# Twelve Newton instructions on VectorE where GpSimd took one power, and a plan sorted anew

## The chip, the core and the metric

The kernel runs on one core of one Trainium2 chip. The metric is device time in microseconds (us) of one execution. Five engines work at once, each through its own queue of instructions in a fixed order: PE (TensorE, matrix products), DVE (VectorE), ACT (ScalarE), POOL (GpSimd) and SP (SyncE, which issues the transfers). An instruction that waits holds up everything behind it on its engine.

## What is computed

Attention with normalised queries and keys over 8 batches of 12 heads, 448 rows of 64 numbers, and then a feed-forward layer on the 3584 x 768 result, all in float32:

```python
def rmsnorm(x, g):
    rms = np.sqrt(np.mean(x * x, axis=-1, keepdims=True) + 1e-06)
    return x / rms * g
q_n, k_n = (rmsnorm(q, g_q), rmsnorm(k, g_k))
scores = scale * np.matmul(q_n, k_n.transpose(0, 1, 3, 2))
attn = np.exp(scores - np.max(scores, axis=-1, keepdims=True))
attn = attn / (np.sum(attn, axis=-1, keepdims=True) + 1e-09)
...
h = x @ w_in            # 768 -> 2048
g = h * np.cos(h)
return (g @ w_out).astype(np.float32)
```

The part that this case touches is the `1 / rms` of the keys of the first two heads.

## The kernel before

The work is cut into 48 units `u`, each a pair of heads. Six pairs make a batch. For a pair the seven blocks of 128 query rows give seven score tiles (`score_plain` or `score`, PE), DVE scales each by the query's inverse root and takes the row minimum (`rowmin`, L553), ACT takes the exponential (`expo`, L561), PE transposes the result (`transp`, L595 to L604), ACT and DVE copy it out of PSUM, and PE multiplies with the values (`av`, `av_plain`). The three score tiles in bank `S` and one in bank `ph` are all that may be open at once for the first pairs, so a later score matmul waits until the exponential has read an earlier tile. The first six pairs run in plain float32; all later ones split each operand in a high and a low part (`pt_high`, `pt_low` and so on). While pairs 6 and up are done, the first feed-forward product of the batch before (`ffn1`, L726 to L728) fills the gaps on PE. After the attention comes the second product, seven block products (`ffn2`, L800 to L802).

Inverse roots are found in two ways of data flow, but by the same instruction. For every pair `st_square` (ACT) and `st_reduce` (DVE) give sums of squares, `r`, and `st_pow` (POOL, L380 and L381) raises them to the power -0.5. The first two pairs are special: their keys come in row by row (`kn_load`; the keys of pair 0 lie in tile `kq`, of pair 1 in tile `kn`), and a short chain normalises and turns them on the chip. It is `kn_square` (ACT, L399), `kn_reduce` (DVE, L405), `kn_pow` (POOL, L409 and L410), `kn_norm` (DVE, L415), `kn_turn` (PE, L420) and `kn_copy` (ACT, L425), which leaves the keys as `kn` with the gains folded in. From pair 2 on the roots go through HBM (`st_store`, `rk_spread`) and POOL multiplies (`k_norm`, L458, giving `km`).

The order of all this is not written out. Each step is registered by `add` with an engine, a cost in us, a due time and the data that it reads and writes. `Plan.order` then plays the program through in its own model of the five engines: whenever an engine is free, it takes, of the steps whose inputs are there, the one that is due first. The steps are emitted in that order, and the chip's queues keep it. `SHIFT` moves the due times of a kind of step by so many us, apart for three stages of the program (pairs 9 and up, pairs 6 to 8, and the first six).

```python
        if name in ("pt_low", "pt_high", "pt_copy", "transp"):
            name += str(args[2])
        elif name == "av" and args[1] == 3:
            name += "3"
        due += SHIFT.get(name, (0.0,) * 3)[stage]
...
        cost *= {DVE: 1.059, ACT: 1.026, POOL: 1.021}.get(eng, 1.0)
        plan.add(eng, cost, due, fn, *args, **more)
```

Of the kernel before, what the change touches and what calls it, by code (L numbers as in the profile page):

```python
# [10 lines left out]
F32 = mybir.dt.float32  # L11
F32R = mybir.dt.float32r
I32 = mybir.dt.int32
AF = mybir.ActivationFunctionType
ALU = mybir.AluOpType
# [5 lines left out]
PE, ACT, DVE, POOL, SP = "PE", "ACT", "DVE", "POOL", "SP"  # L21
# [128 lines left out]
def tile_attention_moe(  # L150
# [11 lines left out]
    nc = tc.nc  # L162
    NU = sd_in.shape[0]
    B, S, D = 8, kq_in.shape[2] - 512, 64
# [11 lines left out]
    KB = S // 4  # L176
# [32 lines left out]
    def g_fold():  # L209
# [5 lines left out]
    wts, wfl, raw = {}, {}, {}  # L215
    RING = {
# [3 lines left out]
    }  # L220

# [94 lines left out]
    pair = {}  # L316
# [37 lines left out]
    def tl(u, name, shape, dt, tag=None):  # L354
        tag = tag or name
        t = pair.setdefault(u, {})[name] = apool.tile(shape, dt, tag=tag, name=f"{name}{u}", bufs=RING[tag])
        return t
# [43 lines left out]
    def kn_reduce(u, a, b):  # L401
        if a == 0:
            tl(u, "rn", [128, 8], F32)
        sq = kn_bank(u)[:KB, 128 * a : 128 * b].rearrange("p (t d) -> p t d", d=D)
        nc.vector.tensor_reduce(pair[u]["rn"][:KB, 2 * a : 2 * b], sq, axis=AX.X, op=ALU.add)  # L405

    def kn_pow(u):
        r = pair[u]["rn"][:KB]
# [266 lines left out]
    xf = {}  # L675
# [141 lines left out]
    def y_store(b, oc, src):  # L817
# [2 lines left out]

    plan = Plan(RING, loose=PKEYS)
    SHIFT = {
        "av": (5.3, 0.0, 0.0), "av3": (3.6, 0.0, 0.0), "av_plain": (0.0, 0.0, 15.8), "e_place": (-4.5, 0.0, 0.0),
        "expo": (8.1, 0.0, 0.0), "ffn1": (0.0, -3.8, 0.0), "h_out": (-4.4, 0.0, 0.0), "k_high": (5.2, 7.1, 0.0),
        "kq_load": (-19.1, 0.0, 0.0), "m_place": (15.1, -13.5, 0.0), "pt_copy0": (0.0, 0.0, -3.9),
        "pt_high1": (-1.8, 0.0, 0.0), "pt_low0": (-20.7, 9.3, 0.0), "pt_low1": (-5.9, 0.0, 0.0),
        "q_high": (5.1, 0.0, 0.0), "q_low": (-2.0, 3.7, 0.0), "q_scale": (-9.4, -8.6, 0.0),
        "rowmin": (10.1, 6.2, 1.1), "rs_copy": (0.0, 2.2, 0.0), "rs_load": (0.0, 0.0, -12.0),
        "rs_store": (6.6, 0.0, 11.5), "rsum": (-8.3, 0.0, 0.0), "st_pow": (-14.6, 0.0, 0.0),
        "st_reduce": (5.3, 0.0, 0.0), "st_square": (2.5, 0.0, 0.0), "transp0": (-4.1, 0.0, 0.0),  # L830
        "transp1": (2.4, -8.7, 0.0), "v_decode": (8.3, 0.0, 0.0), "v_high": (0.0, 12.8, 0.0),
        "v_load": (19.8, -12.8, 0.0), "v_store": (12.5, 0.0, 0.0), "w_decode": (0.4, 0.0, 0.0),
        "x_norm": (4.0, 0.0, 0.0), "x_plain": (0.0, 0.0, -20.3), "x_split": (-3.4, 0.0, 0.0),
        "x_sum": (13.2, 0.0, 0.0),
    }

    def add(eng, cost, due, fn, *args, **more):
        name, first = fn.__name__, args[0] if args else 0
        stage = 0
        if name in ("ffn1", "h_out", "h_store", "h_both", "x_split"):  # L840
            stage = int(first < (NP if name == "x_split" else 1))
        elif name[:2] not in ("w_", "v_", "e_") or name in ("v_load", "v_high", "v_low", "v_plain", "e_place"):
            stage = 2 if first < NP else int(first < NP + 3)
# [5 lines that stand above are left out]
        if name in ("w_load", "w_decode", "w_high", "w_low"):  # L849
            due += -0.414 * first  # L850
        if name in ("ffn1", "h_out", "h_store", "h_both") and not first:
            due += -0.355 * args[1]
        if name in ("v_fetch", "v_decode", "v_sum", "v_split", "v_store"):
            due += 25.441 * first
        cost *= {DVE: 1.059, ACT: 1.026, POOL: 1.021}.get(eng, 1.0)
        plan.add(eng, cost, due, fn, *args, **more)
# [68 lines left out]
    def prepare(u):  # L925
        D0 = base(u)
        kmw = [km_key(u)]
        sd, r, kd, khi, qd, qhi = ([(n, u)] for n in ("sd", "r", "kd", "khi", "qd", "qhi"))
        sd = [("sd", max(u, NKT - 1), u)]
        turned, plain = u < NKT, u < NP  # L930
        if turned:
            kn, rn, kb = [("qd" if u == 0 else "ql", u)], [("rn", u)], [("pt", 0, n) for n in ((0,) if u == 0 else (1, 2))]
            add(SP, ISS, D0 - 60, kn_load, u, w=kn, kb=224.0)
            halves = ((0, 2), (2, 4)) if u == 0 else ((0, 4),)
            hs = [("kn", u, h) for h in halves]
            sh = 1.0 / len(halves)
            for h, k in zip(halves, hs):
                add(ACT, 0.06 + 0.57 * sh, D0 - 50, kn_square, u, *h, r=kn, w=[k, *(kb if h[0] == 0 else [])])
            for h, k in zip(halves, hs):
                add(DVE, 0.06 + 0.63 * sh, D0 - 50, kn_reduce, u, *h, r=[k, *kb], w=[("rn" if h[0] == 0 else "rm", u)])  # L940
            add(POOL, 1.9, D0 - 50, kn_pow, u, r=kb, w=rn + [("rm", u)])
            for h, k in zip(halves, hs):
                add(DVE, 0.06 + 0.63 * sh, D0 - 50, kn_norm, u, *h, r=rn + kn, w=[k])
            for h, k in zip(halves, hs):
                add(PE, 0.98 * sh, D0 - 50, kn_turn, u, *h, r=[k, *kn, *kb], w=[k])
            for n, (h, k) in enumerate(zip(halves, hs)):
                add(ACT, 0.73 if u else (0.36, 0.53)[n], D0 - 50, kn_copy, u, *h, r=[k, *kb, ("gsc", 0)], w=kmw)
        elif plain:
            add(SP, ISS, D0 - 36, k_load, u, w=kd, kb=224.0, start=D0 - 36)
        else:  # L950
            add(SP, ISS, D0 - 34, kq_load, u, w=kd + qd, kb=480.0, start=D0 - 40)
        add(SP, ISS, D0 - 45, st_load, u, w=sd, kb=224.0 if turned else 448.0, start=0.0 if u < NP else D0 - 60)
        if plain:
            add(SP, ISS, D0 - 44 if turned else D0 - 30, q_load, u, w=[("qp", u)], kb=256.0,
                start=0.0 if turned else D0 - 28)
        add(ACT, 0.55 if turned else 0.86, D0 - 40, st_square, u, w=sd)
        add(DVE, 0.7 if turned else 1.08, D0 - 38, st_reduce, u, r=sd, w=r, start=9.0 * (u == 1))
        add(POOL, 2.25 if turned else 2.9, D0 - 34, st_pow, u, w=r)
        if not turned:
            add(SP, ISS, D0 - 30, st_store, u, r=r, w=[("rkd", u)], kb=4.0)  # L960
            if plain:
                add(SP, 2 * ISS, D0 - 26, rk_spread, u, r=[("rkd", u)], w=[("D", u)], kb=224.0)
                add(POOL, 1.55, D0 - 18, k_norm, u, r=[("D", u)] + kd, w=kmw)
            else:
                add(SP, ISS, D0 - 26, rk_load, u, r=[("rkd", u)], w=[("M", u, 2)], kb=224.0)
                add(POOL, 1.13, D0 - 20, k_norm, u, r=[("M", u, 2)], w=kd)
                add(ACT, 0.5, D0 - 17, k_high, u, r=kd, w=khi)
                add(POOL, 1.2, D0 - 15, k_low, u, r=kd + khi, w=[("kl", u)])
        if plain:
            if not turned:  # L970
                add(POOL, 0.8, D0 - 16, q_scale, u, r=[("gsc", 0)], w=[("qp", u)])
            add(SP, ISS, D0 - 12, v_plain, u, w=[("vs", u)], kb=256.0, start=D0 - 6)
            return
        add(POOL, 0.66, D0 - 19, q_scale, u, r=[("gsc", 0)], w=qd)
        add(ACT, 0.52, D0 - 16, q_high, u, r=qd, w=qhi)
        add(POOL, 1.26, D0 - 14, q_low, u, r=qd + qhi, w=[("ql", u)])
        add(SP, 2 * ISS, D0 - 14, m_place, u, 0, r=khi, w=[("M", u, 0)], kb=358.0)
        add(SP, 2 * ISS, D0 - 13.5, d_place, u, r=qhi, w=[("D", u)], kb=614.0)
        add(SP, 2 * ISS, D0 - 13, m_place, u, 1, r=[("kl", u)], w=[("M", u, 1)], kb=358.0)
        add(SP, ISS, D0 - 12.5, e_place, u, r=[("ql", u)], w=[("E", u)], kb=307.0)  # L980
        add(SP, ISS, D0 - 12, v_load, u, w=[("vd", u)], kb=256.0, start=D0 - 22)
        add(POOL, 0.82, D0, v_high, u, r=[("vd", u)], w=[("vs", u)])
        add(POOL, 1.3, D0 + 2, v_low, u, r=[("vd", u)], w=[("vs", u)])
# [160 lines left out]
    add = plan.add  # L1144
# [170 lines left out]
```

## Time and profile before

| | us |
|---|---|
| median of 3 runs | 1373.23 (1372.65 to 1375.12) |
| the profiled execution | 1371.8 |
| its span, first to last instruction | 1370.0 |
| PE busy in the span | 1343.2 (98%) |
| DVE, ACT, POOL busy | 1075.0, 927.4, 632.5 |

The profile comes from one execution, and its 1371.8 us is 1.4 us under the median. PE counts as busy while any matmul is in flight, and its matmuls overlap, so 98% is not 98% of its best rate. The idle time of PE is not spread evenly: about half of it lies in the first 60 us.

### The profile page before, as it was taken

How to read it: one execution, taken by the hardware profiler on the slowest of the kernel's cores; microseconds unless marked ns; L12 is line 12 of the kernel's file. 1: busy time of each engine (PE TensorE's matmuls, PEld its weight loads, DVE VectorE, ACT ScalarE, POOL GpSimd, SP SyncE). 2: the span in 40 equal slices, each digit the busy share in tenths (PEclk: the TensorE clock that was granted, in tenths of full speed). 3: DMA queues.
4: the chain of work that ended last, by engine and by line, in shares of the span. 5: the costliest groups of instructions: out<-in, count | busy, mean ns of one | idle time of the engine just before them, and what ended most of it. 6: DMA issues, size and time to landing. Idle time of an engine off the chain costs nothing.

```text
span 1370.0 us, 21500 instructions
## 1 busy us (share of the span) xinstructions
PE 1343.2 (98%) x6998; PEld 1171.0 (85%) x6998; DVE 1075.0 (78%) x1859; ACT 927.4 (68%) x1872; POOL 632.5 (46%) x554
## 2 busy tenths in 40 slices
PE   7899999999999999999999999999999999999998
PEld 3346888788888989888889888999999999999998
DVE  7888899977787887787877877628889889889742
ACT  6677878777877877777777787638666366366321
POOL 4889978676766866666776584330000000000000
PEclk9999999999999999999999999999999999999999
DMA  6798776889798899798987897338988369369334
GB/s 241 263 276 194 186 170 188 240 232 244 201 260 212 216 243 209 218 243 227 247 209 196 227 233 200 120 131 315 370 298 300 119 246 306 112 247 313 105 113 153
DMA packets 149472, 302.19 MB, mean 221 GB/s; under 512 B 34368, under 2 KB 83088, under 8 KB 149360
## 3 DMA queue, kind: packets, MB, share of 16 engines
q1 hardware_dynamic: 149360, 300.83, 75.2%
q8 instruction: 55, 0.90, 0.3%
q14 instruction: 57, 0.47, 0.1%
HBM read 193.99 MB, written 62.73 MB: 187 GB/s over the span
## 4 chain that ended last, share of the span: by engine, by line
PE 86%; POOL 5%; DVE 3%; DMA 2%; issue 2%; ACT 1%; SPq 0%; POOLq 0%; ACTq 0%; DVEq 0%
PE y L800 10%; PE y L802 10%; PE y L801 10%; PE ph L726 9%; PE ph L727 8%; PE ph L728 8%; PE S L549 8%; PE PT L595 7%; PE O L642 4%; PE O L644 3%; PE O L660 1%; PE S L533 1%; PE y L727 1%; PE y L728 1%; PE y L726 1%
## 5 line engine op out<-in xcount | busy, mean ns | idle before, releaser
L553 DVE TENSOR_SCALAR_CACHE_REDUCE S<-S,r 128x448 f32<-128x448 f32 x336 | 225.3, 686 | 56.4 <-PE S L549 45.4
L561 ACT ACTIVATE P<-S,sm 128x448 f32<-128x448 f32 x336 | 213.3, 637 | 73.8 <-DVE S L553 56.7
L726 PE MATMUL ph<-xs,wi 128*128 128x448 f32 x660 | 251.1, 380 | 1.6 <-ACT hbuf L744 1.6
L800 PE MATMUL y<-g,wo 128*128 128x448 f32 x672 | 245.4, 365 | 0.0
L801 PE MATMUL y<-g,wo 128*128 128x448 f32 x672 | 245.4, 365 | 0.0
L802 PE MATMUL y<-g,wo 128*128 128x448 f32 x672 | 245.4, 365 | 0.0
L727 PE MATMUL ph<-xs,wi 128*128 128x448 f32 x660 | 241.7, 366 | 0.0
L728 PE MATMUL ph<-xs,wi 128*128 128x448 f32 x660 | 241.3, 366 | 0.0
L782 ACT CAST g<-gq 128x896 fp32r<-128x896 f32 x112 | 105.7, 944 | 170.6 <-PE y L802 170.1
L618 ACT CAST hi<-PT 128x512 fp32r<-128x512 f32 (+2 forms) x336 | 175.7, 532 | 63.7 <-PE PT L595 23.8
L625 DVE TENSOR_TENSOR lo<-PT,hi 128x512 fp32r<-128x512 f32 (+1 forms) x252 | 153.2, 619 | 41.2 <-ACT hi L618 39.0
L780 DVE TENSOR_TENSOR g<-gq,g 128x896 fp32r<-128x896 f32 x112 | 122.0, 1089 | 60.2 <-ACT g L782 59.7
L595 PEld LDWEIGHTS PT<-ident,P 128*128 128x128 f32 x1008 | 124.0, 141 | 42.2 <-issue 6.6
L595 PE MATMUL PT<-ident,P 128*128 128x128 f32 x1008 | 155.8, 275 | 2.8 <-DVE rt L574 1.2
L726 PEld LDWEIGHTS ph<-xs,wi 128*128 128x128 f32 x660 | 124.2, 188 | 17.8 <-ACT hbuf L744 3.4
L800 PEld LDWEIGHTS y<-g,wo 128*128 128x128 f32 x672 | 126.2, 188 | 10.0
L802 PEld LDWEIGHTS y<-g,wo 128*128 128x128 f32 x672 | 126.2, 188 | 9.9
L801 PEld LDWEIGHTS y<-g,wo 128*128 128x128 f32 x672 | 126.2, 188 | 9.9
L728 PEld LDWEIGHTS ph<-xs,wi 128*128 128x128 f32 x660 | 124.0, 188 | 10.6
L727 PEld LDWEIGHTS ph<-xs,wi 128*128 128x128 f32 x660 | 124.4, 189 | 8.6
L381 POOL TENSOR_TENSOR r<-r,nhalf 128x14 f32<-128x14 f32 (+1 forms) x48 | 124.5, 2593 | 4.0
L642 PE MATMUL O<-hi,vs 128*128 128x448 f32 x336 | 122.3, 378 | 1.1 <-DVE hi L627 0.8
(129 smaller groups left out, 2635.9 us busy)
## 6 DMA issues: line engine op xcount, KB each, us to landing
wo<-wo_d SPq DMA_DIRECT2D x152, 384.0 KB
gq<-h_d SPq DMA_DIRECT2D x64, 448.0 KB
h_d<-hbuf SPq DMA_DIRECT2D x54, 448.0 KB
wo_d<-ao SPq DMA_DIRECT2D x56, 384.0 KB
sd<-sd SPq DMA_DIRECT2D x46, 448.0 KB
kq<-kq SPq DMA_DIRECT2D x42, 480.0 KB
D<-qhi SPq DMA_DIRECT2D x84, 192.0 KB
raw<-w_in SPq DMA_DIRECT2D x16, 768.0 KB
```

Of the source, the lines that this page charges most:

```text
L553: nc.vector.tensor_scalar(d["S", t][:, :S], d["S", t][:, :S], d["r"][:, t : t + 1], None, op0=ALU.mult, op1=ALU.min, accum_out=d["sm"][:, ...
L561: nc.scalar.activation(p_rows(u, t), d.pop(("S", t))[:, :S], AF.Exp, bias=sm[:, 1, t : t + 1], scale=-1.0, accum_out=sm[:, 2, t : t + 1],)
L595: nc.tensor.transpose(pt[part][:, i * 128 : i * 128 + 128], p_rows(u, t)[:, c : c + 128], ident)
L618: nc.scalar.copy(hi if kc < 3 else hi[:64], pt_rows(u, kc, part))
L625: nc.vector.tensor_tensor(lo, src, hi.bitcast(F32), ALU.subtract)
L642: nc.tensor.matmul(O, st, d["hi", kc][:, HEADS[hh]], start=(kc == 0), stop=(kc == 3))
L726: nc.tensor.matmul(ph[:, :S], whi, x2[:, 0, :], start=(cc == 0), stop=False)
L727: nc.tensor.matmul(ph[:, :S], whi, x2[:, 1, :], start=False, stop=False)
L728: nc.tensor.matmul(ph[:, :S], wlo, x2[:, 0, :], start=False, stop=(cc == NCC - 1))
L800: nc.tensor.matmul(y, whi, hi[:, e], start=first and e == 0, stop=False, **more)
L801: nc.tensor.matmul(y, whi, lo[:, e], start=False, stop=False, **more)
L802: nc.tensor.matmul(y, wlo, hi[:, e], start=False, stop=last and e == NG - 1, **more)
```

## The change

Pair 0 alone gets `kn_root` in place of `kn_pow`. It adds the epsilon on DVE, makes a first guess of the inverse root from the bits of the number (shift, multiply by -1, add a constant), and improves it in three Newton steps of three instructions. That is twelve DVE instructions on 112 x 8 numbers, each of which reads what the one before it wrote. The plan counts them as one step of 0.85 us. Pair 1 keeps `kn_pow`. Two small tiles are added. In `SHIFT` six entries become zero, in whole or in one stage: `e_place`, `ffn1`, `pt_low0`, `q_low`, `rowmin` (first six pairs) and `transp1`; the rest stand as before.

```diff
+    def kn_root(u):
+        x = pair[u]["rn"][:KB]
+        y, t = (tl(u, name, [128, 8], F32)[:KB] for name in ("ry", "rt8"))
+        nc.vector.tensor_scalar(x, x, D * 1e-6, 3.0e38, op0=ALU.add, op1=ALU.min)
+        nc.vector.tensor_scalar(
+            y.bitcast(I32), x.bitcast(I32), 1, 0x7FFFFFFF, op0=ALU.logical_shift_right, op1=ALU.bitwise_and
+        )
+        nc.vector.tensor_scalar(y.bitcast(I32), y.bitcast(I32), -1.0, 1597463007.0, op0=ALU.mult, op1=ALU.add)
+        for last in (False, False, True):
+            nc.vector.tensor_tensor(t, x, y, ALU.mult)
+            nc.vector.scalar_tensor_tensor(t, t, -0.5, y, op0=ALU.mult, op1=ALU.mult)
+            nc.vector.scalar_tensor_tensor(x if last else y, t, 1.5, y, op0=ALU.add, op1=ALU.mult)
...
-        "pt_low0": (-20.7, 9.3, 0.0), "pt_low1": (-5.9, 0.0, 0.0),
+        "pt_low0": (0.0, 9.3, 0.0), "pt_low1": (-5.9, 0.0, 0.0), "q_high": (5.1, 0.0, 0.0),
...
-            add(POOL, 1.9, D0 - 50, kn_pow, u, r=kb, w=rn + [("rm", u)])
+            if u:
+                add(POOL, 1.9, D0 - 50, kn_pow, u, r=kb, w=rn + [("rm", u)])
+            else:
+                add(DVE, 0.85, D0 - 50, kn_root, u, r=kb, w=rn + [("rm", u)])
```

What this does to the queues is seen at the start on three engines. In the changed kernel the lines after L405 stand 13 further down: `kn_norm` is L428, `kn_copy` L438, `rowmin` L566 and `expo` L574.

On POOL, at the start of the program; `rn_127` is the sums of pair 0's keys, `rn_145` (in the changed kernel `rn_151`) those of pair 1, `r_137` and `r_155` (`r_157` and `r_176`) the sums of the queries of pairs 0 and 1. Before:

```order
L409 TENSOR_SCALAR rn_127<-rn_127 112x8
L410 TENSOR_TENSOR rn_127<-rn_127,nhalf 112x8
L380 TENSOR_SCALAR r_137<-r_137 128x7
L381 TENSOR_TENSOR r_137<-r_137,nhalf 128x7
L409 TENSOR_SCALAR rn_145<-rn_145 112x8
L410 TENSOR_TENSOR rn_145<-rn_145,nhalf 112x8
L380 TENSOR_SCALAR r_155<-r_155 128x7
L381 TENSOR_TENSOR r_155<-r_155,nhalf 128x7
```

And in the changed kernel, on POOL at the same place:

```order
L422 TENSOR_SCALAR rn_151<-rn_151 112x8
L423 TENSOR_TENSOR rn_151<-rn_151,nhalf 112x8
L380 TENSOR_SCALAR r_157<-r_157 128x7
L381 TENSOR_TENSOR r_157<-r_157,nhalf 128x7
L380 TENSOR_SCALAR r_176<-r_176 128x7
L381 TENSOR_TENSOR r_176<-r_176,nhalf 128x7
```

The power for pair 0's keys is gone, and that for pair 1's keys now stands ahead of that for pair 0's queries, where it stood behind it.

On DVE, from the first instruction after the sums of pair 0's keys; `sd` holds squares of queries, and `S_0` is the first score tile. Before:

```order
L375 TENSOR_REDUCE r_137<-sd_119 128x7
L415 TENSOR_TENSOR kq<-kq,rn_127 112x256 x2
L405 TENSOR_REDUCE rn_145<-PT_111 112x8
L375 TENSOR_REDUCE r_155<-sd_119 128x7
L553 TENSOR_SCALAR S_0_162,sm_161<-S_0_162,r_137 128x448
L415 TENSOR_TENSOR kn_117<-kn_117,rn_145 112x512
L553 TENSOR_SCALAR S_4_163,sm_161<-S_4_163,r_137 128x448
```

And in the changed kernel, on DVE from the last of the twelve new instructions:

```order
L418 SCALAR_TENSOR_TENSOR rn_127<-rt_133,ry_132 112x8
L428 TENSOR_TENSOR kq<-kq,rn_127 112x256 x2
L405 TENSOR_REDUCE rn_151<-PT_111 112x8
L375 TENSOR_REDUCE r_157<-sd_119 128x7
L375 TENSOR_REDUCE r_176<-sd_119 128x7
L428 TENSOR_TENSOR kn_117<-kn_117,rn_151 112x512
L566 TENSOR_SCALAR S_0_169,sm_168<-S_0_169,r_157 128x448
```

The sums of pair 0's queries moved from ahead of `kn_norm` to behind the sums of pair 1's keys, and pair 1's `kn_norm` moved ahead of the first row minimum.

On ACT, from the copy of pair 0's keys on; `kn_102` and `kn_103` are the turned keys of pairs 0 and 1, `P` the exponentials. Before:

```order
L372 ACTIVATE sd_119<-sd_119 128x448 x2
L425 ACTIVATE kn_102<-PT_110,gs 128x224 x2
L425 ACTIVATE kn_102<-PT_110,gs 64x64
L561 ACTIVATE P,sm_161<-S_0_162,sm_161 128x448
L561 ACTIVATE P,sm_161<-S_4_163,sm_161 128x448
L561 ACTIVATE P,sm_161<-S_1_170,sm_161 128x448
L425 ACTIVATE kn_103<-PT_111,gs 128x448
L425 ACTIVATE kn_103<-PT_111,gs 64x64
L561 ACTIVATE P,sm_161<-S_5_171,sm_161 128x448
```

And in the changed kernel, on ACT at the same place:

```order
L372 ACTIVATE sd_119<-sd_119 128x448
L438 ACTIVATE kn_102<-PT_110,gs 128x224 x2
L438 ACTIVATE kn_102<-PT_110,gs 64x64
L372 ACTIVATE sd_119<-sd_119 128x448
L438 ACTIVATE kn_103<-PT_111,gs 128x448
L438 ACTIVATE kn_103<-PT_111,gs 64x64
L574 ACTIVATE P,sm_168<-S_0_169,sm_168 128x448
L574 ACTIVATE P,sm_168<-S_4_170,sm_168 128x448
```

The copy of pair 1's keys stood behind three exponentials of pair 0 and now stands ahead of all seven. PE's order at the start is the same in both. Apart from these places all five queues are the same up to the work of pair 6, some 115 us in; from there to the last pair many steps stand a few rows earlier or later, and then the queues are equal again to the end.

## Rows read from the trace of the kernel before

**Rows 1.** The page's first part: busy time of each engine, share of the span and instructions.

```profile
PE 1343.2 (98%) x6998; PEld 1171.0 (85%) x6998; DVE 1075.0 (78%) x1859; ACT 927.4 (68%) x1872; POOL 632.5 (46%) x554
```

**Rows 2.** Busy time by stretch: the stretch in us and its length, then busy us and instruction count of PE, PE's weight loads, DVE, ACT and POOL, then the granted clock of PE, the busy share of the transfer engines, and GB/s.

```profile
20.00:40.00 20.00, 20.00 (x92) 8.74 (x91) 18.35 (x35) 14.57 (x30) 13.33 (x10) 1.00 0.68 226
40.00:52.00 12.00, 7.31 (x20) 2.49 (x19) 10.30 (x22) 7.53 (x19) 11.51 (x12) 1.00 0.78 277
52.00:56.00 4.00, 4.00 (x13) 1.86 (x11) 3.16 (x7) 3.12 (x7) 1.19 (x1) 0.57 0.78 305
56.00:115.00 59.00, 58.81 (x273) 30.06 (x272) 51.61 (x103) 44.44 (x103) 51.16 (x43) 1.00 0.90 252
```

**Rows 3.** Instructions in order of time at the start, all engines: start in us, duration in us (of all, where xN says how many), engine, line, operation, tiles, shapes, and in brackets the idle time before and what ended it.

```profile
4.30 0.75 DVE L405 TENSOR_REDUCE rn<-PT 112x4 f32<-112x256 f32 x2 [0.51 <-ACT PT L399]
...
5.43 1.66 POOL L410 TENSOR_TENSOR rn<-rn,nhalf 112x8 f32<-112x8 f32 x1
...
6.69 0.62 DVE L375 TENSOR_REDUCE r<-sd 128x7 f32<-128x448 f32 x1 [1.63 <-ACT sd L372]
7.23 0.75 DVE L415 TENSOR_TENSOR kq<-kq,rn 112x256 f32<-112x256 f32 x2
...
7.40 0.31 POOL L380 TENSOR_SCALAR r<-r 128x7 f32<-128x7 f32 x1 [0.31 <-DVE r L375]
...
7.74 0.98 PE L420 MATMUL PT<-ident,kq 112*128 112x112 f32 x4 [7.74 <-DVE kq L415]
7.80 1.53 POOL L381 TENSOR_TENSOR r<-r,nhalf 128x7 f32<-128x7 f32 x1
8.01 0.69 DVE L405 TENSOR_REDUCE rn<-PT 112x8 f32<-112x512 f32 x1
...
8.81 1.12 ACT L425 ACTIVATE kn<-PT,gs 128x224 f32<-128x224 f32 x3 [0.84 <-PE PT L420]
...
9.41 0.21 POOL L409 TENSOR_SCALAR rn<-rn 112x8 f32<-112x8 f32 x1
...
9.70 1.63 POOL L410 TENSOR_TENSOR rn<-rn,nhalf 112x8 f32<-112x8 f32 x1
```

**Rows 4.** DVE's instructions of the first 60 us grouped by line and shape: count, busy us in all, mean ns of one, idle time before.

```profile
L415 DVE TENSOR_TENSOR kq<-kq,rn 112x256 f32<-112x256 f32 x2 | 0.8, 416 | 0.0
...
L415 DVE TENSOR_TENSOR kn<-kn,rn 112x512 f32<-112x512 f32 x1 | 0.7, 689 | 0.0
L571 DVE RECIPROCAL sm<-sm 128x7 f32<-128x7 f32 x3 | 0.6, 197 | 0.6 <-ACT sm L569 0.6
...
L210 DVE SCALAR_TENSOR_TENSOR gs<-gs 128x2 f32<-128x2 f32 x1 | 0.2, 161 | 2.8 <-DMA gs<-gg 2.8
```

**Rows 5.** DVE in order of time, a stretch in which each of three instructions reads what the one before it wrote (`decode`); columns as in rows 3.

```profile
36.16 0.54 DVE L244 TENSOR_SCALAR wf<-raw 128x768 int32<-128x768 int32 x1
36.74 0.96 DVE L246 SCALAR_TENSOR_TENSOR wf<-raw,wf 128x768 int32<-128x768 int32 x1
37.73 0.96 DVE L248 SCALAR_TENSOR_TENSOR wf<-raw,wf 128x768 int32<-128x768 int32 x1
```

**Rows 6.** The work of pair 0 in order of time, engines as named; columns as in rows 3.

```profile
9.65 3.69 PE L533 MATMUL S<-kn,q 64*128 64x448 f32 x8 [0.93 <-ACT kn L425]
...
11.65 0.69 DVE L553 TENSOR_SCALAR_CACHE_REDUCE S<-S,r 128x448 f32<-128x448 f32 x1 [2.42 <-POOL r L380]
...
12.44 0.63 ACT L561 ACTIVATE P<-S,sm 128x448 f32<-128x448 f32 x1 [2.50 <-DVE S L553]
...
13.27 1.01 PE L420 MATMUL PT<-ident,kn 112*128 112x112 f32 x4
...
14.88 0.95 ACT L425 ACTIVATE kn<-PT,gs 128x448 f32<-128x448 f32 x2
...
16.48 0.62 ACT L561 ACTIVATE P<-S,sm 128x448 f32<-128x448 f32 x1
...
17.09 0.63 ACT L561 ACTIVATE P<-S,sm 128x448 f32<-128x448 f32 x1
...
17.70 0.64 ACT L561 ACTIVATE P<-S,sm 128x448 f32<-128x448 f32 x1
```

**Rows 7.** POOL in order of time before the keys of pair 2 are ready; columns as in rows 3.

```profile
34.35 0.22 POOL L380 TENSOR_SCALAR r<-r 128x14 f32<-128x14 f32 x1 [0.99 <-DVE r L375]
...
40.62 2.24 POOL L458 TENSOR_TENSOR km<-kq,D 128x448 f32<-128x448 f32 x2
```

**Rows 8.** PE in order of time around there; columns as in rows 3.

```profile
42.51 2.16 PE L533 MATMUL S<-km,q 64*128 64x448 f32 x8 [1.71 <-POOL km L458]
45.17 1.02 PE L533 MATMUL S<-km,q 64*128 64x448 f32 x2 [0.50 <-ACT P L561]
...
50.64 0.64 PE L533 MATMUL S<-km,q 64*128 64x448 f32 x1 [1.84 <-POOL km L458]
```

**Rows 9.** Busy time by stretch in the rest of the program; columns as in rows 2.

```profile
115.00:150.00 35.00, 30.87 (x165) 25.77 (x165) 32.82 (x67) 29.54 (x68) 34.59 (x28) 1.00 0.82 179
150.00:280.00 130.00, 126.16 (x688) 110.28 (x687) 118.41 (x220) 100.94 (x230) 100.19 (x83) 1.00 0.76 198
280.00:500.00 220.00, 220.00 (x1222) 197.35 (x1221) 175.89 (x373) 172.81 (x405) 152.39 (x136) 1.00 0.86 231
...
870.00:1300.00 430.00, 430.00 (x2137) 397.83 (x2136) 342.93 (x368) 245.71 (x305) 17.11 (x15) 1.00 0.67 233
```

More of the change, by code (lines that the diff above doesn't have):

```diff
@@ L822, in tile_attention_moe @@
     SHIFT = {
[L823 to L834, printed above, removed]
+        "av": (5.3, 0.0, 0.0), "av3": (3.6, 0.0, 0.0), "av_plain": (0.0, 0.0, 15.8), "expo": (8.1, 0.0, 0.0),
+        "h_out": (-4.4, 0.0, 0.0), "k_high": (5.2, 7.1, 0.0), "kq_load": (-19.1, 0.0, 0.0),
+        "m_place": (15.1, -13.5, 0.0), "pt_copy0": (0.0, 0.0, -3.9), "pt_high1": (-1.8, 0.0, 0.0),
+        "pt_low0": (0.0, 9.3, 0.0), "pt_low1": (-5.9, 0.0, 0.0), "q_high": (5.1, 0.0, 0.0),
+        "q_low": (-2.0, 0.0, 0.0), "q_scale": (-9.4, -8.6, 0.0), "rowmin": (10.1, 6.2, 0.0),
+        "rs_copy": (0.0, 2.2, 0.0), "rs_load": (0.0, 0.0, -12.0), "rs_store": (6.6, 0.0, 11.5),
+        "rsum": (-8.3, 0.0, 0.0), "st_pow": (-14.6, 0.0, 0.0), "st_reduce": (5.3, 0.0, 0.0),
+        "st_square": (2.5, 0.0, 0.0), "transp0": (-4.1, 0.0, 0.0), "transp1": (2.4, 0.0, 0.0),
+        "v_decode": (8.3, 0.0, 0.0), "v_high": (0.0, 12.8, 0.0), "v_load": (19.8, -12.8, 0.0),
+        "v_store": (12.5, 0.0, 0.0), "w_decode": (0.4, 0.0, 0.0), "x_norm": (4.0, 0.0, 0.0),
+        "x_plain": (0.0, 0.0, -20.3), "x_split": (-3.4, 0.0, 0.0), "x_sum": (13.2, 0.0, 0.0),
     }
```

2 rows, old and new, of the table RING are left out of this document.

## The prediction

> **What bounds the kernel now.** I read the page's busy times first: PE is busy 98% of the span [rows 1], so the end moves only by PE's idle time or by what slows it. The busy times by stretch show where that is. From 870 to 1300 us PE is busy all 430 us with 2137 matmuls, one each 0.20 us [rows 9]; the queues are unchanged there, so nothing is to be had. From 280 to 500 us it is busy throughout as well. PE idles 4.1 us between 115 and 150, 3.8 us between 150 and 280 [rows 9], and 4.7 us between 40 and 52 [rows 2]. Then the instructions in order of time: PE does nothing until 7.74 us [rows 3], because pair 0's keys must be normalised and turned first. That opening is what the change works on. A delay there reaches the end if everything behind it hangs on it, so the last view is the chain of pair 2's keys on POOL [rows 7] and PE's wait for them [rows 8].
>
> **The part that is removed.** The sums of pair 0's keys are done at 4.30 + 0.75 = 5.05 us, POOL's power at 5.43 + 1.66 = 7.09, and the normalising on DVE starts at 7.23 [rows 3]. From 5.05 to 7.23 is 2.18 us, and the last 0.14 of it is not POOL's: DVE is in the sums of pair 0's queries, 6.69 + 0.62 = 7.31, and starts the next instruction 0.08 early. So 2.18 us is all that twelve instructions have to beat.
>
> **The part that is added.** The trace has no DVE instruction of 112x8 with these operations; the duration comes from two neighbours. One on 128x2 takes 161 ns; between 256 and 512 numbers the same instruction goes from 416 to 689 ns, 273/256 = 1.07 ns a number [rows 4]. Eight numbers then take 161 + 6 x 1.07 = 167 ns. The step between them: where an instruction needs the result before it, it starts after that one's end. 36.16 + 0.54 = 36.70, next start 36.74; 36.74 + 0.96 = 37.70, next start 37.73 [rows 5]; 0.035 us. Instructions that need nothing of each other overlap: two of 0.416 take 0.75 together [rows 3, 4], so 0.08 us are saved. All twelve need the one before. 12 x (0.167 + 0.035) = 2.42 us after a gap of 0.035: normalising starts at 5.05 + 0.035 + 2.42 = 7.50, 0.27 us later than now. Bounds: if they overlapped, 12 x (0.161 - 0.08) = 0.97 us, that is 1.2 us earlier than now; if each took as long as the reciprocal on 7 numbers, 0.197 us [rows 4], 12 x 0.232 = 2.78 us, 0.6 us later. I take the middle one, which rests on the nearest rows.
>
> [...]
>
> **The part that is moved, at the start.** Everything of pair 0 behind the normalising comes 0.27 us later: its end 7.98 becomes 8.25, the turning on PE 7.74 becomes 8.01, the copy on ACT 8.81 becomes 9.08 [rows 3], the first scores 9.65 become 9.92 [rows 6]. Now the new places in the queues. DVE takes the sums of pair 1's keys at 8.01 + 0.27 = 8.28, ending 8.97, and the sums of pair 0's queries, which lay under POOL's power before, behind them. On POOL the power for pair 1's keys is now first: from 9.41 to 9.70 + 1.63 = 11.33 it takes 1.92 us [rows 3], so 9.06 to 10.98. The power for pair 0's queries, 7.40 to 9.33 before [rows 3], 1.93 us, runs 11.06 to 12.99. The first row minimum, which starts at 11.65 now when its score tile is ready [rows 6], must wait for it: 13.02, 1.37 us later. Queued behind it on DVE are the other minima.
>
> On ACT the copy of pair 1's keys stands ahead of all seven exponentials. It waits for pair 1's turning on PE, which follows pair 0's first eight score instructions: 13.27 [rows 6] becomes 13.54, ending 14.55; the copy takes 0.95 [rows 6], to about 15.6. The first exponential, 12.44 before, starts at 15.62. Seven at a pitch of 0.61 (16.48, 17.09, 17.70 [rows 6]) put the last one at 15.62 + 3.66 = 19.28 against 17.70: 1.6 us later. Before, three exponentials were done by the time that copy started, at 14.88. There is a wait more: the fifth score tile needs the first tile's place in PSUM, free at 15.62 + 0.63 + 0.1 = 16.35. Its matmuls take 1.02 alone [rows 8], its minimum 0.69 [rows 6], so its exponential is ready at about 18.15 against its turn at 18.06, and the two after it follow later still, up to 0.5 us in all. The start costs 1.6 to 2.1 us; I take 1.9. POOL is freed of 1.9 us at a place where it idles anyway.
>
> **Does it reach the end?** From 20 to 40 us PE is busy all 20.00 us [rows 2], so it cannot catch up. The keys of pair 2 are made on POOL at 40.62, and PE waits 1.71 us for them [rows 8]. POOL itself had idled 0.99 us until DVE's sums at 34.35 [rows 7], and these follow PE's results of pair 0. All of it hangs on the delayed work, with the same queues. From 56 to 115 PE is busy 58.81 of 59 us [rows 2]. I count nothing as absorbed; at most the 1 us of POOL's idling and some of the 0.2 us could be, were transfers the real bound.
>
> **The due times.** From about 115 us the queues differ by a few rows. Where PE idles most, 4.1 + 3.8 us between 115 and 280 [rows 9], the new order may do better by half, 4 us, or worse by as much. From 280 to 870 it can hardly gain and can lose 1 or 2 us. I put it at zero, with -4 and +5 as ends.
>
> **The sum.** 1371.8 of the profiled execution + 1.9 = 1373.7. The median shown is 1373.23, 1.4 above that execution, so the forecast is 1375.1 against the median: 0.14% slower, which is inside the 0.2% (2.75 us, 1370.5 to 1376.0) about which a measurement of this kernel can tell nothing from no change.
>
> **The rivals.**
> First, the new order wins: three or so of the 7.9 us of idle time between 115 and 280 go. 1371.8 + 1.9 - 4 + 1.4 = 1371. For it speaks that these idle spells are the largest left behind the start; against it, that only a few rows move and PE's work is the same. Chance 0.18.
>
> Second, slower: PE's clock. PE has a hole from 14.55, when pair 1's keys are turned, to 16.35, when the first score place is free, and works thinly until 20. [...] Chance for this side 0.28.
>
> Third, the change does what its plan says: the twelve overlap and take 0.97 us. Normalising starts at 6.05. Then POOL's powers end at 9.8 and 11.8, pair 1's turning, held by the eight score instructions from 8.47 on, starts at 12.1, and its copy ends at 14.15. Seven exponentials from there put the last at 14.2 + 3.66 = 17.85, and with the wait for PSUM 18.3, against 17.70. So even this case gains nothing, because of ACT's new order: 1371.8 + 0.4 + 1.4 = 1373.6. Chance 0.12.
>
> **How the numbers follow.** The forecast has 0.42, at 1375.1 with its own range 1373 to 1377. Of that I give 0.33 to within 0.2% and 0.09 to slower. The second rival is slower with all its 0.28, the third within with its 0.12, and the first splits, 0.09 faster and 0.09 within. Together faster 0.09, within 0.54, slower 0.37. The range reaches into both sides: 1371.0 leaves out about half of the first rival, 1379.0 the tail of the second.
>
> **What would show it.** In the profile after: twelve DVE instructions of 160 to 170 ns with 0.035 us between them, and normalising at 7.5 us; the first row minimum near 13.0 and released by POOL; the copy of pair 1's keys ahead of the first exponential, which starts near 15.6; the last exponential of pair 0 near 19.5; the keys of pair 2 about 2 us later than 40.62, and PE's wait for them as long as before. The third rival shows as normalising near 6 us, the second as a granted clock under 1.00 between 15 and 25 us, the first as less idle time on PE between 115 and 280 us. I am wrong in the main point if pair 2's keys come no later than now, for then something in front of them absorbs the delay.

## The result, and the profile after

The changed kernel took 1386.64 us in the median (1382.80 to 1390.84), the kernel before on the same chip 1374.17 (1372.65 to 1376.40). The ratio is 1.0094, with an interval of 1.0076 to 1.0113: 12.5 us slower. The four times lie in two places, 1382.80 and 1383.36, and 1389.93 and 1390.84; the profile below is of the execution of 1383.36.

The start first, all engines in order of time, as [rows 3, 6]:

```profile
4.25 0.76 DVE L405 TENSOR_REDUCE rn<-PT 112x4 f32<-112x256 f32 x2 [0.51 <-ACT PT L399]
5.04 0.17 DVE L410 TENSOR_SCALAR rn<-rn 112x8 f32<-112x8 f32 x1
5.24 0.17 DVE L411 TENSOR_SCALAR ry<-rn 112x8 int32<-112x8 int32 x1
...
7.26 0.17 DVE L418 SCALAR_TENSOR_TENSOR rn<-rt,ry 112x8 f32<-112x8 f32 x1
7.46 0.76 DVE L428 TENSOR_TENSOR kq<-kq,rn 112x256 f32<-112x256 f32 x2
...
12.95 0.69 DVE L566 TENSOR_SCALAR_CACHE_REDUCE S<-S,r 128x448 f32<-128x448 f32 x1 [0.77 <-POOL r L381]
...
14.32 0.96 ACT L438 ACTIVATE kn<-PT,gs 128x448 f32<-128x448 f32 x2 [3.39 <-PE PT L433]
...
15.31 0.63 ACT L574 ACTIVATE P<-S,sm 128x448 f32<-128x448 f32 x1
...
16.08 5.65 PE L546 MATMUL S<-kn,q 64*128 64x448 f32 x10 [1.80 <-ACT P L574]
...
20.76 0.64 ACT L574 ACTIVATE P<-S,sm 128x448 f32<-128x448 f32 x1 [1.07 <-DVE S L566]
...
21.66 1.75 PE L608 MATMUL PT<-ident,P 128*128 128x128 f32 x7
```

Up to 15.31 us this is what was forecast: twelve instructions 0.2 us apart, normalising at 7.46, the first row minimum at 12.95 after POOL's root, the first exponential at 15.31. Then it is not. Ten score matmuls that wait for the exponentials' places in PSUM take 5.65 us, the last exponential starts at 20.76 where 17.70 stood before [rows 6], and PE turns the first results at 21.66. In the kernel before, these rows of PE read:

```profile
14.21 2.26 PE L533 MATMUL S<-kn,q 64*128 64x448 f32 x6
16.64 1.63 PE L533 MATMUL S<-kn,q 64*128 64x448 f32 x4 [0.17 <-ACT P L561]
18.20 0.98 PE L595 MATMUL PT<-ident,P 128*128 128x128 f32 x7
```

So the start lost 21.66 - 18.20 = 3.5 us. The keys of pair 2, and PE's wait for them, as [rows 7, 8]:

```profile
45.13 2.24 POOL L471 TENSOR_TENSOR km<-kq,D 128x448 f32<-128x448 f32 x2
...
47.03 3.82 PE L546 MATMUL S<-km,q 64*128 64x448 f32 x9 [1.70 <-POOL km L471]
```

They come 4.5 us later than at 40.62, and the wait for them, 1.70, is as long as it was. Nothing in front of them took the delay up.

Busy time by stretch, as [rows 2, 9]; the columns are those of [rows 2]:

```profile
14.21:17.10 2.89, 1.09 (x4) 0.59 (x4) 1.72 (x7) 2.74 (x8) 0.56 (x1) 1.00 0.97 381
17.10:24.00 6.90, 6.90 (x17) 2.86 (x17) 5.21 (x13) 3.71 (x13) 0.00 (x0) 0.51 0.10 39
...
56.00:115.00 59.00, 58.46 (x253) 27.49 (x252) 52.38 (x106) 45.18 (x105) 46.15 (x40) 0.95 0.90 255
115.00:150.00 35.00, 32.23 (x177) 27.38 (x176) 31.83 (x62) 27.32 (x63) 34.67 (x28) 1.00 0.85 196
150.00:280.00 130.00, 124.00 (x673) 109.40 (x672) 118.57 (x218) 101.14 (x227) 101.96 (x84) 0.99 0.73 193
280.00:500.00 220.00, 218.48 (x1211) 195.46 (x1210) 178.15 (x372) 171.18 (x404) 157.33 (x138) 1.00 0.86 227
870.00:1300.00 430.00, 428.62 (x2125) 394.34 (x2124) 345.01 (x380) 248.85 (x319) 19.76 (x18) 1.00 0.67 235
```

Two things stand out. From 17.10 to 24.00 the granted clock of PE is 0.51, right after PE was busy only 1.09 of 2.89 us. And the last stretch, in which PE never waited before, holds 12 matmuls less, 2125 against 2137 [rows 9]. The queues there are the same, so this was the place where I had said that nothing could change.

It has two causes: PE is idle for 1.4 of the 430 us, and something else that cannot be seen as a wait. The stretch from 910 to 960 us, in which PE is busy throughout in both, of the kernel before:

```profile
910.00:960.00 50.00, 50.00 (x249) 46.34 (x248) 31.34 (x31) 32.17 (x45) 3.02 (x3) 1.00 0.79 278
```

and of the changed kernel:

```profile
910.00:960.00 50.00, 50.00 (x244) 45.41 (x243) 17.75 (x21) 23.16 (x32) 6.97 (x7) 1.00 0.61 223
1100.00:1200.00 100.00, 100.00 (x495) 92.67 (x494) 85.48 (x89) 58.22 (x66) 0.00 (x0) 1.00 0.64 221
```

Same clock, no idle time, 244 matmuls in place of 249. By the starts in the trace, the kernel before repeats steps of 203, 202, 203, 199 and 207 ns from 893 us to the end, 202.7 on average. The changed kernel repeats 207, 207 and 206, 206.7 on average, from about 904 to 967 us, where PE pauses by 0.3 us; behind that it runs at 202.7 too. Four nanoseconds are little, but some 2300 matmuls follow, and 2300 x 4.0 = 9.2 us.

### The profile page after: what moved, and what is told of

It reads as the page before. It is cut to its first block, busy times and chain, and to the rows that moved or that the text cites. A ratio compares the mean times of both kernels' runs of the same rounds, so it can differ in the third digit from the quotient of the medians.

```text
span 1381.6 us, 21522 instructions
## 1 busy us (share of the span) xinstructions
PE 1350.0 (98%) x6998; PEld 1174.2 (85%) x6998; DVE 1086.6 (79%) x1871; ACT 927.6 (67%) x1872; POOL 633.5 (46%) x552
## 5 line engine op out<-in xcount | busy, mean ns | idle before, releaser
L566 DVE TENSOR_SCALAR_CACHE_REDUCE S<-S,r 128x448 f32<-128x448 f32 x336 | 226.2, 686 | 61.2 <-PE S L562 47.7
L574 ACT ACTIVATE P<-S,sm 128x448 f32<-128x448 f32 x336 | 213.7, 638 | 81.4 <-DVE S L566 65.8
```

Source lines behind the costliest of these rows:

```text
L566: nc.vector.tensor_scalar(d["S", t][:, :S], d["S", t][:, :S], d["r"][:, t : t + 1], None, op0=ALU.mult, op1=ALU.min, accum_out=d["sm"][:, ...
L574: nc.scalar.activation(p_rows(u, t), d.pop(("S", t))[:, :S], AF.Exp, bias=sm[:, 1, t : t + 1], scale=-1.0, accum_out=sm[:, 2, t : t + 1],)
```

## The experiments

**First four: the start, the order behind it, and the twelve, apart.** Each composes its sequence of steps out of the plan of the kernel before (`old`) and of the changed one (`new`): `joined(x, 60.0, y)` takes what `x` starts in the first 60 us of the plan and the rest in the order of `y`.

```diff
-seq = new.seq
+seq = joined(new.seq, 60.0, old.seq)                       # a_start_only
+seq = joined(old.seq, 60.0, new.seq)                       # b_late_only
+seq = using(old.seq, kn_root)                              # c_twelve_only
+seq = using(joined(new.seq, 60.0, old.seq), kn_pow)        # d_start_order_pow
```

> The changed kernel's queues up to 60 us of the plan (the twelve instructions, and the new order on DVE, ACT and POOL), and behind them the queues of the kernel before. Theory (the start costs 4.5 to 5.3 us by 65 us, by the exponentials standing behind the copy of pair 1's keys and by the slower clock that follows, and the rest of the loss is the later order's): about 5 us over the kernel before, 1379, with a granted clock under 1.00 between 15 and 25 us. Rival (the whole loss comes from the start, since a late start also delays the preparation of w_out): 10 us or more over it. Rival (the start's loss is absorbed later): within 2 us of it.

> The start of the kernel before (the power on GpSimd), and from 60 us of the plan on the queues of the changed kernel. Theory: the later order costs by itself what the traces show behind 225 us, 3.2 us between 225 and 330 and 3.2 us between 900 and 1005, together 6 us: 1380. Rival (those losses come only with a late start): no more than 2 us over the kernel before.

> All queues of the kernel before, with the twelve instructions in place of the power for pair 0's keys and nothing else moved. Theory (the order, not the instructions, makes the start late): the sums of pair 0's queries now stand behind the twelve, so normalising starts at 7.43 + 0.53 = 7.96, 0.73 us later than before, and the last exponential of pair 0 is later by as much; total 0.5 to 1 us over the kernel before. Rival (the twelve instructions themselves make the start late): 4 us or more.

> The changed kernel's queue order up to 60 us, but the inverse root made by the power on GpSimd as before; behind it the queues of the kernel before. Theory (the order makes the start late): normalising starts near 7.1 us, and still the first exponential not before 15.2 us, the last of pair 0 near 20.5; 4 to 5 us over the kernel before. Rival (the twelve instructions make the start late): within 1 us of the kernel before.

The times, beside 1373.78 for the kernel before: the start 1388.02 (ratio 1.0090, 1.0074 to 1.0106), the late order 1379.47 (1.0042, 1.0017 to 1.0067), the twelve alone 1382.94 (1.0059, 1.0039 to 1.0080), the new start with the power still on GpSimd 1377.07 (1.0020, 1.0006 to 1.0034). The start alone is 9 us above the 1379 of its theory, the late order near its 1380. The surprise is the twelve alone: normalising 0.8 us later, everything else as before, and 9 us lost where 0.5 to 1 was expected. The first half of that run's trace lies about 1 us behind the kernel before; from 895 us on it loses 0.40 us with every 100 matmuls:

```profile
910.00:960.00 50.00, 50.00 (x244) 45.41 (x243) 29.86 (x30) 31.52 (x43) 3.02 (x3) 1.00 0.74 261
1100.00:1200.00 100.00, 100.00 (x485) 90.81 (x485) 86.16 (x91) 57.27 (x65) 0.00 (x0) 1.00 0.65 223
```

It keeps the slow pitch (the mean step from one matmul to the next) to the end, 485 matmuls in 100 us against 495. The start-only kernel does so as well (486). The two with the power on GpSimd have the fast one (495 each). The late order's ten times spread from 1375.30 to 1390.51, so its 1379.47 says little by itself.

**Second four: what sets the pitch.** With the twelve instructions come two things that no diff of the order shows. Their scratch tiles take 64 bytes in SBUF, and everything allocated behind them moves up: the tiles `r`, `vs`, `sm`, `wf`, `hi`, `rs`, `xf` and some more. The tiles that the last 2300 matmuls read, `xs`, `wi`, `g` and `wo`, do not move. And PE's queue holds one more wait instruction, ahead of the transposes at the start.

```diff
+        if u == 0:                                         # e_pow_with_tiles, in kn_pow
+            for name in ("ry", "rt8"):
+                tl(u, name, [128, 8], F32)
...
-        y, t = (tl(u, name, [128, 8], F32)[:KB] for name in ("ry", "rt8"))
+        z = pbuf[:KB, RING["P"] - 1]                       # f_twelve_old_place, in kn_root
+        y, t = z[:, :8], z[:, 8:16]
...
-        for j in range(a, b):
+        for j in [*range(a, b)] + [b - 1] * (u == 0 and b == 2):   # g and h, in kn_turn
```

> The kernel before, with the power on GpSimd and its own queues, except that the two 32-byte tiles that the twelve instructions use are allocated and left unused, so that the addresses in SBUF are those of the run with the twelve instructions alone (1382.9 us). In that run the last 2300 matmuls came 206.7 ns apart and in the kernel before 202.7 ns apart. Theory S (the addresses of the tiles set the pitch): 1382 to 1384, and 206.7 ns. Theory P (the one instruction more that TensorE has in its queue, a wait, sets it): 1373 to 1375, and 202.7 ns. Theory T (the pitch follows from the timing of the last stall ahead of the stream): 202.7 ns, since nothing is timed otherwise.

> The twelve instructions alone in the old queues, but their two scratch tiles lie in a part of the buffer of P that is not yet in use, so that every address in SBUF is that of the kernel before. TensorE's queue still has its one wait more. Theory S: 202.7 ns and 1374 to 1375.5 (the twelve alone put the start back by 1 us). Theory P: 206.7 ns and 1382 to 1384. Theory T: 206.7 ns, as in the run with the twelve alone, which had the same timing.

> The kernel before with one instruction more on TensorE: the second transpose of pair 0's normalised keys is made twice (about 0.1 us at 8 us from the start). Addresses as before. Theory P: 206.7 ns and 1382 to 1384, so that one matmul of 0.1 us costs 9 us. Theory S: 202.7 ns and 1373.5 to 1375. Theory T: either.

> The twelve alone in the old queues, with their own tiles, and the same transpose made twice. Theory S: 206.7 ns and 1382 to 1384. Theory P, if an even count is the fast one: 202.7 ns and 1374 to 1376; if the count matters in another way, 206.7 ns still. Theory T: either.

The kernel before with 64 unused bytes took 1384.24 (ratio 1.0073, 1.0058 to 1.0088). The twelve instructions with every address as before took 1375.03 (1.0001, 0.9991 to 1.0011). One transpose more cost nothing without the tiles (1373.72) and changed nothing with them (1383.82). Two lines are enough to see it, the first of the kernel with the power and unused tiles:

```profile
1100.00:1200.00 100.00, 100.00 (x486) 90.81 (x485) 86.03 (x90) 56.78 (x66) 0.00 (x0) 1.00 0.63 220
```

and this one of the kernel with the twelve in the old addresses:

```profile
1100.00:1200.00 100.00, 100.00 (x496) 92.68 (x495) 85.96 (x90) 57.73 (x66) 0.00 (x0) 1.00 0.64 223
```

All four came out as the theory of the addresses says, within 0.3 us of its ranges. PE's extra instruction and the timing of the start are out. The twelve instructions themselves cost nothing that can be measured.

**Third four: the whole change without it, the late stores, and the pause.**

```diff
+        z = pbuf[:KB, RING["P"] - 1]                       # i_change_old_place: the changed kernel
...
+        if n == 0 and o == 0:                              # k_twelve_pause, in ffn2
+            nc.tensor.transpose(y[:, :128], ident, ident)
+            nc.vector.tensor_copy(y[:, 128:136], y[:, :8])
...
+            if name == "hi" and "pad" not in pads:         # l_pow_hi_moved, in p_tile
+                for n in ("pad", "pad2"):
+                    pads[n] = apool.tile([128, 8], F32, tag=n, name=n, bufs=1)
...
+    NEW_SHIFT["ffn1"] = (0.0, -3.8, 0.0)                   # m_change_ffn1_due, with i's z
```

> The changed kernel, order and all, with the two scratch tiles of the twelve instructions laid in a part of the buffer of P that is not yet in use, so that every address in SBUF is that of the kernel before. If the addresses are what makes the last 2300 matmuls slow, none of them comes at 206.7 ns, the runs near 1390 are gone, and the time is that of the order alone: the new order after 60 us was 1379.5 alone and the new start 1377.1 alone, together 1379 to 1382.5. If the rhythm comes from the order too, 1383 to 1387 as the changed kernel.

> The twelve alone in the old queues with their own tiles (1382.9 us, 206.7 ns from 895 us to the end), and one pause of TensorE put in at the first matmul of the second layer's products, near 1000 us: it transposes the identity into the bank that it is about to open, VectorE copies eight columns of it within the bank, and TensorE has to wait for that. Addresses unchanged. If the pitch is a rhythm that lasts until something interrupts it (no tile that the last 2300 matmuls read has moved in SBUF), the pause can end it: 202.7 ns behind it, and 1382.9 - 7.4 + 1 = 1376.5. If the addresses hold the pitch all the time, 206.7 ns behind it too, and 1384. If the pause falls back into the same rhythm by chance, also 1384.

> The kernel before, with 64 unused bytes allocated just ahead of the tiles hi: hi and what lies behind it (rs, xf, vd, qhi, khi, kl, ao) move by 64 bytes, vs, r, sm and wf stay. The matmuls that run just before the slow stream begins read hi and vs. If hi is the tile that sets it, 206.7 ns and 1382 to 1384; if vs (or r, sm, wf), 202.7 ns and 1373.5 to 1375.

> The changed kernel with addresses as before, and with one due time put back: -3.8 for the first layer's matmuls in the first stage. By the plan's own clock the stores of the prepared second weights between 640 and 880 us then come 13 us earlier than in the kernel before, where in the changed kernel they come 16 us later. If those late stores are what costs the 3 us between 900 and 1003 us, this is 3 us faster than the changed kernel with addresses as before: 1376 to 1379.5. If they have nothing to do with it, the same time as that one.

With the old addresses the changed kernel takes 1381.74 (ratio 1.0063, 1.0043 to 1.0083), 4.9 us less than the change as it is. The two intervals overlap, and the medians mix runs of two kinds: two of four near 1390 there, one of six here, at 1389.40. Without these the medians differ by 1.9 us, so how much of the 4.9 the addresses cost this kernel is not settled. The trace of another of its runs shows why that can be: it enters the last stream in the fast rhythm, falls into the slow one at a pause near 967 us and leaves it again at another near 1000. The pause at 967 is a wait for prepared second weights, as PE in order of time shows:

```profile
967.28 0.47 PE L814 MATMUL y<-g,wo 128*128 128x448 f32 x1 [1.50 <-DMA wo<-wo_d]
```

The run with a pause put in, which comes at 961 us, has the slow rhythm ahead of it and the fast one behind it, and took 1378.22 (1.0044, 1.0024 to 1.0064) where it was 1382.94 without:

```profile
910.00:960.00 50.00, 50.00 (x244) 45.44 (x243) 28.90 (x29) 30.74 (x42) 3.02 (x3) 1.00 0.73 255
1100.00:1200.00 100.00, 100.00 (x495) 92.80 (x494) 86.66 (x91) 57.37 (x65) 0.00 (x0) 1.00 0.65 228
```

So the pitch is a rhythm that lasts until something comes between, and a pause can switch it either way or leave it: the changed kernel's pause near 1000 us leaves the fast one. Of the ten runs with the pause put in two are at 1388.51 and 1388.90, so it does not always help; no trace of one was taken. Moving `hi` and what lies behind it cost nothing (1373.91).

The late stores: with one due time put back the changed kernel takes 1378.16 (1.0031, 1.0020 to 1.0042), 3.6 us less. SP's own rows show them. Stores of the prepared weights to DRAM and the first load of them, in the kernel before:

```profile
916.52 4.31 SPq L313 DMA_DIRECT2D wo_d<-ao  x2
...
928.74 0.32 SPq L790 DMA_DIRECT2D wo<-wo_d  x1
```

in the changed kernel:

```profile
925.21 12.24 SPq L313 DMA_DIRECT2D wo_d<-ao  x4
...
945.77 0.32 SPq L803 DMA_DIRECT2D wo<-wo_d  x1
```

and with the due time put back:

```profile
924.84 4.33 SPq L313 DMA_DIRECT2D wo_d<-ao  x2
...
937.11 0.32 SPq L804 DMA_DIRECT2D wo<-wo_d  x1
```

In the changed kernel SP is still issuing stores at 937 us, and its first load comes 17.0 us later than in the kernel before, where it stands at 928.74; here it comes 8.4 later, which is what PE itself is late by. The two stores that were left over stood in front of the loads. The plan's clock had promised more, stores 13 us earlier than in the kernel before; on the chip they came in step with the rest.

That the stores are all of the 3.6 us is not shown. By the starts of the matmuls, the changed kernel with the old addresses falls 2.8 us further behind the kernel before after 900 us (two pauses, and the slow rhythm between them); with the due time put back it falls behind by nothing there and has no pause. And a pause need not be a wait for a load: the long one in the changed kernel's profiled run, near 1000 us, is ended by DVE, as PE's waits between 870 and 1300 us show (what waits, what ended it, us in all, how often, the longest):

```profile
PE y L813 <- DVE outs L826: 1.2, 1, 1.2
```

**Last three: the remaining 4 us, and the tile.**

```diff
+seq = using(joined(old.seq, 60.0, new.seq), kn_root)       # n_change_old_start, on top of m
...
+copy1 = next(s for s in new.seq if s[2] is kn_copy and s[3][0] == 1)      # o_change_copy_later, on top of m
+third = [s for s in new.seq if s[2] is expo and s[3][0] == 0][2]
+seq = [s for s in new.seq if s is not copy1]
+seq.insert(seq.index(third) + 1, copy1)
...
+        if u == 0:                                         # p_pow_vs_moved, in v_plain
+            for n in ("pad", "pad2"):
+                tl(u, n, [128, 8], F32)
```

> The changed kernel with addresses as before and the due time of the first layer's matmuls put back (1378.2 us), now also with the first 60 us in the order of the kernel before, the twelve instructions in the power's place. If what is left above the kernel before is the order of the start, 1373.5 to 1375.5. If the new order behind 60 us still costs something, 1376 to 1378.

> The same kernel of 1378.2 us with the new start, in which only ScalarE's copy of pair 1's keys goes back behind pair 0's third exponential, where the kernel before has it. If that copy in front of the exponentials is what costs the start, 1374 to 1376, and the granted clock reaches full speed near 14.5 us in place of 23 us. If it is GpSimd's order (pair 1's power ahead of pair 0's query root, so that the first row minimum comes late), 1377 to 1379 still.

> The kernel before with 64 unused bytes allocated just ahead of the tiles vs: vs, sm, wf, hi and what lies behind them move, the tiles r stay. Moving hi and what lies behind it alone cost nothing. If vs (the weights of the matmuls just ahead of the last stream; sm and wf are no operands there) sets the rhythm, 206.7 ns and 1383 to 1385. If the tiles r do, 202.7 ns and 1373.5 to 1375.

With the old start 1375.05 (ratio 1.0007, 0.9998 to 1.0015): the order behind the start then costs nothing that can be told. With the new start and only ScalarE's copy of pair 1's keys back behind the third exponential 1374.67 (1.0008, 0.9998 to 1.0018). By the medians, that one instruction's place is 3.5 us. The start of that kernel:

```profile
13.82 0.64 ACT L575 ACTIVATE P<-S,sm 128x448 f32<-128x448 f32 x1 [2.81 <-DVE S L567]
...
14.60 2.58 PE L547 MATMUL S<-kn,q 64*128 64x448 f32 x6
...
17.43 1.63 PE L547 MATMUL S<-kn,q 64*128 64x448 f32 x4 [0.25 <-ACT P L575]
18.50 0.64 ACT L575 ACTIVATE P<-S,sm 128x448 f32<-128x448 f32 x1
18.99 0.98 PE L609 MATMUL PT<-ident,P 128*128 128x128 f32 x7
```

The first exponential starts 1.4 us later than before, because POOL's order is still the new one. But there is no hole on PE, the ten score matmuls run as before, and PE turns the first results at 18.99, 0.8 us late in place of 3.5. Moving `vs`, `sm` and `wf` with the rest took 1382.87 (1.0068, 1.0052 to 1.0085) and 486 matmuls in 100 us. `hi` alone did nothing; of `vs`, `sm` and `wf` the matmuls read `vs` last ahead of the stream, at 892.43 us in the kernel before, and `sm` at 884.6.

`vs` was not moved by itself, but the starts of the matmuls in the 17 traces show the place. Just ahead of the last two matmuls that read `hi` and `vs`, PE is in the slow rhythm in the fast kernels too, in every trace but that with `hi` moved. Where `vs` has its old address, the steps into, between and out of these two are 200 to 203 ns (with `hi` moved 195 to 203), and the fast rhythm follows, in ten traces of ten. Where `vs` has moved, they are 203 to 205 ns, the next step is 213 or 214, and the slow rhythm goes on, in seven of seven. So the kernels part at the two matmuls that read `vs`.

No kernel tried beats the one before.

## Why the prediction was wrong

The forecast was 1375.1, at most 1379.0. The runs split the 12.5 us: 4.9 for the addresses (changed kernel less the same with the old addresses), 3.6 for the late stores, 3.5 for the place of one copy, and 0.5 that cannot be told from nothing. These are differences of medians; the 4.9 rests on how many runs fell near 1390. A single trace cannot be split so finely: the kernel with one transpose more, whose median is as before, falls 4.2 us behind in its trace.

- **The part that is removed, the part that is added: right.** Twelve instructions of 166 to 172 ns, 0.034 us between them, normalising at 7.46 against 7.50 forecast. In the order of before they cost nothing that shows (1.0001).
- **Nothing is to be had, or lost, from 870 us on: wrong, and by the medians the largest error.** The sentence that failed is "the queues are unchanged there, so nothing is to be had". I took unchanged queues for unchanged time. The step from the diff to the cost had no place for where tiles lie in SBUF. The two scratch tiles were in the diff, in `RING` and in `kn_root`; their 64 bytes move `vs`, and in two kernels that kept the power on GpSimd such a shift brought the 9 us, and with the old addresses the twelve instructions were spared them. In the changed kernel's profiled run the slow rhythm lasted from 904 to 967 us, some 300 matmuls or 1.2 us. In the runs near 1390 it would have lasted to the end, 1990 x 4.0 = 8.0 us more, and 1383.36 + 8.0 = 1391.4 is where they are; no trace of one was taken, so that is not shown.
- **The start costs 1.9: mis-sized; it cost 3.5.** The order of events was right up to the first exponential, 15.31 against 15.62. I had seen the hole that the copy makes on PE, from 14.55 to 16.35 by my count and 14.28 to 16.08 in the trace. I left what follows to the second rival: after it the clock is granted at 0.51 for 6.9 us, where [rows 2] have 0.57 for 4 us after the thin stretch. By those rows the price of such a stretch is 0.43 x 4 = 1.7 us, an estimate; added to 1.9 it gives 3.6, as measured at the end, but in part by luck: the slow clock lasted 6.9 us in place of 4, and the trace is 4.5 us late by the keys of pair 2. The chance of 0.28 was too small, because the rows already showed such a hole followed by such a stretch. That the copy's place is the cause and POOL's order is not, the kernel with the copy put back shows; the clock's own share was not tried by itself, and in some traces with the new start no clock is recorded ahead of 22 us. There the ten matmuls are as slow, 6.06 us in the run with the due time put back.
- **Does it reach the end: right.** The keys of pair 2 came 4.5 us late and the wait for them stayed at 1.70.
- **The due times at zero: wrong by 3.6**, inside the +5 that I had as an end. The place was wrong too: I looked at PE's idle time between 115 and 280 us, which grew by 0.8 us in the profiled run; another 1.5 us came between 280 and 500. What the due time of `ffn1` gives back lies, in the traces, behind 900 us, at the pauses near 967 and 1000 us, where SP's stores are late. The plan's own clock had it: in the changed plan the stores between 640 and 880 us stand 16 us later than in the old one, and the last of all at 947.8 in place of 932.5.
- **First and third rival: fell.** There was no less idle time, 2.8 + 6.0 us between 115 and 280 against 7.9, and the twelve did not overlap. The third rival's sum takes 0.4 where its own 18.3 against 17.70 gives 0.6; its 1373.6 would be 1373.8, which changes nothing.

## What to carry to other kernels

A new tile is not free because it is small: it moves what is allocated behind it, and on a stream that is bound by one engine a few nanoseconds an instruction add up to more than the edit (here 4.0 ns a matmul over some 2300 matmuls, 9.2 us). Put scratch where nothing moves, or run the old kernel once with the new tile left unused, before any time is put down to the new instructions. Where an instruction is moved ahead of others on a busy queue, follow the places in PSUM that those others free: here that made a hole of 1.8 us on PE, 6.9 us at a granted clock of 0.51 came behind it, and the start was 3.5 us late.

## What was not expected of the hardware

Uninterrupted matmuls of the same shape, at a granted clock of 1.00 and with no wait, have two steady rhythms here, 202.7 and 206.7 ns on average. Which one is taken depends on the matmuls and pauses just ahead: two matmuls that read another tile end the slow rhythm or leave it, with 64 bytes in that tile's address (at the old address the fast one follows in ten traces of ten, at the new one the slow one goes on in seven of seven). The slow one then lasts for up to 2300 matmuls: with the twelve instructions alone, 244 in 50 us from 910 us on and 485 in 100 us from 1100 us on, where the kernel with the old addresses has 249 and 496.
